# Decoding the first two expert weight blocks in two parts at the seam between attention and the expert layers

## The chip, the cores and the metric

The kernel runs on one core of one Trainium2 chip. The metric is the device time of one execution in microseconds; lower is better. A core has TensorE (PE, with its weight loads shown as PEld), VectorE (DVE), ScalarE (ACT), GpSimd (POOL) and SyncE (SP, which here only issues DMAs).

## The reference

A clustered attention feeds two expert layers, all in float32.

```python
# q, k, v: (2, 8, 768, 64); centroids: (8, 16, 64)
mask = argmax(q_n . c_n) == argmax(k_n . c_n)      # same nearest centroid
attn = softmax(where(mask, q k^T / 8, -1e9))
x = (attn @ v) as 1536 tokens x 512
# layer 1: w_in 512x2048, w_out 2048x512
x = max(0.01 h, h) @ w_out   with h = x @ w_in
# layer 2: same shapes
out = relu(h)**2 @ w_out     with h = x @ w_in
```

## The kernel before

**Numbers.** Every float32 product is made of three TensorE products of a high and a low part (`xh`, `xl`; `wh`, `wl`; `gh`, `gl`), so each operand is split: a copy rounds to the high part, a subtraction gives the low one.

**Attention.** There are 8 pairs of heads (NP), and each pair has 6 units (UPP) of 256 queries, 48 units (NU) in all. A unit has the scores `S` (line 438), their row maximum `nm` on DVE (460), the exponential `e` on ACT (470), the reciprocal `r` of the row sums (484), the normalisation on POOL (487), twelve transposes into PSUM `T` (500), the split of `T` into `eh` on ACT (511) and `el` on DVE (517), the product with the values into `A` (535), and the fold of `A` into `xt` on ACT (548) and DVE (557). When a pair is done, POOL splits `xt` into `xh` and `xl` (215, 565). `r_t[u]` holds a unit's row sums, `xt_t[p]` a pair's result.

**Experts.** 2048 hidden columns are taken in blocks of 128; a block is one tile of 128 x 1024 words, whose columns 0 to 511 are w_in and 512 to 1023 are w_out. The host passes each word as 64 bits of a wider format, so a block is a load `wraw` of 1024 KB (line 157) and a decode in seven pieces (`decode_pieces`): the load, `mag` on ACT (166), `shift`, `low` and `sign` on DVE (170, 176, 183), the high part `wh` on ACT and the low part `wl` on POOL (143, 144). There is one `wraw` buffer, so a block's load waits for the sign piece of the one before it.

For a pair of blocks, three groups of 512 tokens (b = 0, 1, 2) go through `unit(b, j)`: 12 matmuls of block j's w_in into one bank of `h` (line 865), then ACT and DVE split the activated result (908, 909, 914); and through `out_of(b, j)`: 12 matmuls of block j's w_out into four banks `o` (943). The first pair's sequence is unit(0,0), unit(0,1), unit(1,0), out_of(0,0), unit(1,1), out_of(0,1), unit(2,0), out_of(1,0), unit(2,1), out_of(1,1); the remaining two outputs come in the next pair's sequence. Group 0 needs attention pairs 0 to 3 alone; groups 1 and 2 need the last pair too, in the last three of a unit's 12 matmuls.

**Buffers.** PSUM has eight banks. The four of `h` are those of attention's `S`, three of `o` are those of `T`, and the fourth is that of `A`. SBUF of attention is given on, tile by tile, to pools opened after it. `stg[0]` holds `wraw` and one `wt`; `stg[1]`, opened after attention, another `wt` and `ws`.

**Order.** Attention up to its last six units is ordered by hand (`PLAN`). From there (`manual.close()`) the compiler's planner orders PE, DVE, ACT and POOL by its own model of the times, until `(m, f) == (0, 2)`, the second pair of blocks, where a hand order begins again (`order`). Instructions of a hand-ordered stretch keep their order among themselves on their engine; the planner places others around them. SP's DMAs keep the order in which they are written throughout. The pieces of the first block (`early`) are written one after another into attention's last six units; the pieces of the second after unit(0,0); its load is held, by a small POOL copy into its buffer, until the row sums of the third unit from the end exist. `TURN` says after which step of a pair which pieces of the next pair's blocks are written.

Of the kernel before, what the change touches and what calls it, by code (L numbers as in the profile page):

```python
# [18 lines left out]
W_SHIFT = float(2.0 ** -112)  # L19
# [45 lines left out]
def attention_moe_moe_kernel(  # L65
# [9 lines left out]
    nc = tc.nc  # L75
    NP, _, _, S = qk.shape
# [10 lines left out]
    N = 512  # L87
    NBLK = NT // N
    PLAIN = (3, 1)
    EARLY = 1  # L90
    RING = 6
    SIDE = 4

# [54 lines left out]
    def decode_pieces(ci):  # L148
# [3 lines left out]

        def load():
            st["raw"] = stg[0].tile([128, 2 * DM, 2], I32, tag="wraw", name="wraw")
            if ci == EARLY:
                pool_copy(out=st["raw"][:, 0].bitcast(F32), in_=r_t[NU - 3])
            nc.sync.dma_start(
                out=st["raw"].rearrange("p a b -> p (a b)"), in_=(w1, w2)[m][f + j].bitcast(I32)
            )

        def mag():
            pool = stg[0] if j == 0 or ci < 2 else stg[1]
# [26 lines left out]
            st["rest"] = split_block(ci, st["t"].bitcast(F32))  # L189

        return [load, mag, shift, low, sign, high, lambda: st["rest"]()]

    def sum_pieces(ci):

# [936 lines left out]
    def step_list(m, f, prev):  # L1131
# [30 lines left out]
        ((0, 1),), ((0, 2), (0, 3)), ((0, 4), (1, 0)), ((0, 5),), ((0, 6), (1, 1)),  # L1162
        ((1, 2), (1, 3)), ((1, 4), (2, 0)), ((1, 5), (1, 6), (3, 0)), ((2, 1),), ((2, 2),),
    )
    TURN_LAST = TURN[:9] + (
        TURN[9] + ((3, 1),), ((3, 2), (3, 3)), ((3, 4), (4, 0)), (),
    )
# [38 lines left out]
    for m in range(2):  # L1206
        turn = 0
        for f in range(0, NF, 2):
            if (m, f) == (0, 2):
                order.enter_context(  # L1210
                    tc.manual_schedule(
                        engines={
                            mybir.EngineType.PE,
                            mybir.EngineType.DVE,
                            mybir.EngineType.Activation,
                            mybir.EngineType.Pool,
                        }
                    )
                )
# [3 lines left out]
            for i, step in enumerate(seq):  # L1223
                step()
# [58 lines left out]
```

## Time and profile before

| | |
|---|---|
| time, median of 3 runs | 752.58 us (752.48 to 757.84) |
| the profiled execution: its own time | 753.01 us |
| its span, first to last instruction | 751.2 us |
| PE busy | 743.3 us, 99% |
| DVE, ACT, POOL busy | 573.1, 442.5, 404.7 us |

Matmul ends are modelled in the trace: a matmul of 512 columns shows as 390 ns but the next starts 227 ns after it, so starts and not busy times tell how dense PE is.

### The profile page before, as it was taken

Reading aid. Unit: us, or ns where it says so; the run is one execution under the profiler, and the core shown is the slowest. Engines: PE = TensorE matmul, PEld = TensorE weight load, DVE = VectorE, ACT = ScalarE, POOL = GpSimd, SP = SyncE. Lnnn points to the kernel's source line nnn. Section 1 sums busy time; section 2 is a strip of 40 time slices with the busy share of each in tenths; the row PEclk is TensorE's granted clock in tenths of the full one; section 3 lists DMA queues with packets and bytes.
Section 4 is the critical chain, followed back from the end, with each engine's and each line's share of the span. In section 5 each row is a group of like instructions: output and inputs, shape, how many; then the busy total and the mean of one; then the engine's idle time right before and its main releaser. Section 6 shows DMA issues by size and latency. Waiting matters only on the chain.

```text
span 751.2 us, 11081 instructions
## 1 busy us (share of the span) xinstructions
PE 743.3 (99%) x4044; PEld 647.6 (86%) x4044; DVE 573.1 (76%) x864; ACT 442.5 (59%) x816; POOL 404.7 (54%) x379
## 2 busy tenths in 40 slices
PE   9999999999989999999999999999999999999998
PEld 8999999999988888888888888888788888888886
DVE  7999999999998545877666576686868677686755
ACT  7988988988987564444444344547644445444430
POOL 6999999999856316551442414399242341423400
PEclk9999999999999999999999999999999999999999
DMA  3684574473503212111121112211112211122004
GB/s 108 174 215 113 117 175 114 114 175 74 151 0 113 87 38 101 56 57 57 60 110 57 56 57 63 106 57 56 57 57 84 84 57 56 57 89 79 1 1 168
DMA packets 16406, 64.78 MB, mean 86 GB/s; under 512 B 3040, under 2 KB 4192, under 8 KB 11360
## 3 DMA queue, kind: packets, MB, share of 16 engines
q1 hardware_dynamic: 16352, 64.07, 28.6%
q8 instruction: 32, 0.52, 0.3%
q14 instruction: 22, 0.18, 0.1%
HBM read 43.02 MB, written 3.15 MB: 61 GB/s over the span
## 4 chain that ended last, share of the span: by engine, by line
PE 90%; DVE 5%; ACT 4%; issue 1%; POOL 0%; DMA 0%; POOLq 0%; DVEq 0%; ACTq 0%
PE o L943 33%; PE h L865 32%; PE A L535 8%; PE S L438 7%; PE T L500 7%; ACT e L470 2%; PE S L311 1%; DVE nm L460 1%; DVE el L517 1%; ACT eh L511 1%; DVE xl L1127 1%; PE o L973 1%; PE dots L311 0%; DVE wt L176 0%; ACT wt L166 0%
## 5 line engine op out<-in xcount | busy, mean ns | idle before, releaser
L144 POOL TENSOR_TENSOR wl<-wt,wh 128x1024 fp32r<-128x1024 f32 x32 | 76.8, 2401 | 128.2 <-ACT wh L143 128.2
L914 DVE TENSOR_TENSOR gl<-h,gh 128x512 fp32r<-128x512 f32 x96 | 65.6, 690 | 71.2 <-ACT h L909 52.7
L865 PE MATMUL h<-xh,wh 128*128 128x512 f32 x288 | 112.2, 391 | 0.2
L865 PE MATMUL h<-xl,wh 128*128 128x512 f32 x288 | 112.2, 389 | 0.0
L865 PE MATMUL h<-xh,wl 128*128 128x512 f32 x288 | 112.0, 389 | 0.0
L985 DVE TENSOR_TENSOR acc<-o,acc 128x512 f32<-128x512 f32 x144 | 92.8, 684 | 12.8 <-PE o L943 12.8
L487 POOL TENSOR_SCALAR e<-e,r 128x768 f32<-128x768 f32 x96 | 89.0, 937 | 17.4 <-DVE r L484 13.2
L517 DVE TENSOR_TENSOR el<-T,eh 128x512 fp32r<-128x512 f32 x144 | 94.5, 682 | 3.3 <-ACT eh L511 2.0
L470 ACT ACTIVATE e<-S,nm 128x768 f32<-128x768 f32 x96 | 87.1, 908 | 11.2 <-DVE ds L339 5.2
L460 DVE TENSOR_REDUCE nm<-S 128x1 f32<-128x768 f32 x96 | 90.7, 947 | 3.9 <-PE S L311 2.0
L438 PE MATMUL S<-hb 128*128 128x384 f32 (+1 forms) x384 | 90.4, 350 | 1.3 <-ACT e L470 1.0
L511 ACT CAST eh<-T 128x512 fp32r<-128x512 f32 x144 | 79.7, 588 | 9.9 <-PE T L500 9.6
L500 PE MATMUL T<-ident,e 128*128 128x128 f32 x576 | 81.1, 274 | 0.9 <-POOL e L487 0.8
L535 PE MATMUL A<-eh,vv 128*128 128x256 f32 x288 | 80.0, 307 | 0.7 <-DVE xt L557 0.7
L207 POOL TENSOR_TENSOR ws<-wt 128x256 f32<-128x256 f32 x24 | 17.8, 741 | 110.8 <-DVE wt L183 110.8
L943 PE MATMUL o<-gl,wh 128*128 128x512 f32 x192 | 74.7, 389 | 0.0
L943 PE MATMUL o<-gh,wl 128*128 128x512 f32 x192 | 74.7, 389 | 0.0
L943 PE MATMUL o<-gh,wh 128*128 128x512 f32 x192 | 73.4, 389 | 0.0
L500 PEld LDWEIGHTS T<-ident,e 128*128 128x128 f32 x576 | 68.9, 143 | 5.1 <-POOL e L487 1.1
L535 PE MATMUL A<-el,vv 128*128 128x256 f32 x288 | 72.9, 283 | 0.0
L943 PE MATMUL o<-wh,gh 128*128 128x512 f32 x184 | 71.6, 389 | 0.0
L943 PE MATMUL o<-wl,gh 128*128 128x512 f32 x184 | 71.6, 389 | 0.0
(162 smaller groups left out, 1629.3 us busy)
## 6 DMA issues: line engine op xcount, KB each, us to landing
wraw<-w SPq DMA_DIRECT2D x32, 1024.0 KB, 4.7
hb<-spl SPq DMA_DIRECT2D x14, 576.0 KB, 4.7
hb<-spl SPq DMA_DIRECT2D x42, 192.0 KB, 5.1
rqk<-qk SPq DMA_DIRECT2D x16, 384.0 KB, 3.7
rv<-v SPq DMA_DIRECT2D x8, 384.0 KB, 3.2
out<-q SPq DMA_DIRECT2D x11, 256.0 KB, 2.0
hb<-st SPq DMA_DIRECT2D x56, 24.0 KB, 2.0
out<-q SPq DMA_DIRECT2D x2, 128.0 KB, 1.8
```

The lines of the kernel that those rows point to most:

```text
L144: return lambda: nc.gpsimd.tensor_tensor(out=wl, in0=t, in1=wh.bitcast(F32), op=ALU.subtract)
L438: nc.tensor.matmul(out=s[:, c, 0:HALF], lhsT=hb[0:k, a, i * 128 : (i + 1) * 128], rhs=hb[0:k, b, c * HALF : (c + 1) * HALF], start=(a == 0 ...
L460: nc.vector.tensor_reduce(out=n, in_=s_t[t][:, :, 0:HALF], axis=AX.XY, op=ALU.max, negate=True)
L470: nc.scalar.activation(out=e.rearrange("p (a b) -> p a b", a=2), in_=s_t.pop(t)[:, :, 0:HALF], func=AF.Exp, bias=n_t.pop(t), scale=1.0, ac ...
L487: nc.gpsimd.tensor_scalar(out=e_t[t], in0=e_t[t], scalar1=r_t[t // 2][:, t % 2 : t % 2 + 1], scalar2=1.0, op0=ALU.mult, op1=ALU.mult,)
L500: nc.tensor.transpose(T[:, o : o + 128], e_t[2 * u + b][:, kc * 128 : (kc + 1) * 128], ident)
L511: nc.scalar.copy(out=eh[:, 2 * g : 2 * g + 2, :].rearrange("p a b -> p (a b)"), in_=T_t[u, g])
L517: nc.vector.tensor_tensor(out=el[:, 2 * g : 2 * g + 2, :].rearrange("p a b -> p (a b)"), in0=T_t.pop((u, g)), in1=eh[:, 2 * g : 2 * g + 2, ...
L535: nc.tensor.matmul(out=A, lhsT=w, rhs=m[:, kc, :], start=(kc == 0 and i == 0), stop=(kc == KC - 1 and i == 1),)
L865: nc.tensor.matmul(out=out, lhsT=l, rhs=r, start=(first and i == 0), stop=(i == n - 1), skip_group_check=not first,)
L943: nc.tensor.matmul(out=outs[o], lhsT=l, rhs=r, start=(first and i == 0), stop=(last and i == 2),)
L985: nc.vector.tensor_tensor(out=a, in0=ps, in1=a, op=ALU.add)
```

## The change

The first two blocks of layer 1 are no longer decoded whole. `first_pieces(part)` decodes one half of a block: part 0 is w_in, part 1 is w_out, 512 KB each. The halves of part 0 (blocks 0 and 1) share one `wraw` buffer, of which the second is held by the copy from `r_t[NU - 3]`. The w_out half of block 0 then takes that buffer again; the w_out half of block 1 has buffers of `stg[1]`, and its load is held by a POOL copy from columns 256 to 257 of the last pair's `xt`, which the last unit but one writes. The pieces are written so: w_in of block 0 in attention's last six units; after unit(0,0), w_in of block 1, w_out of block 0, and the load of the third block; before step 3 of the first pair, out_of(0,0), the w_out of block 1. The hand order begins at that step 3 instead of at the second pair, and the first pair's sequence has a table of its own, `TURN_FIRST`.

```diff
         def load():
             st["raw"] = stg[0].tile([128, 2 * DM, 2], I32, tag="wraw", name="wraw")
-            if ci == EARLY:
-                pool_copy(out=st["raw"][:, 0].bitcast(F32), in_=r_t[NU - 3])
...
+    def first_pieces(part):
+
+        st = {}
+        cols = slice(part * DM, (part + 1) * DM)
+
+        def load(b):
+            if (part, b) == (1, 1):
+                raw = stg[1].tile([128, DM, 2], I32, tag="ws", name="wraw")
+                t = stg[1].tile([128, 2 * DM], I32, tag="wt", name="wt")[:, 0:DM]
+                pool_copy(out=raw[:, 0].bitcast(F32), in_=x_end[0][:, 256:258])
+            else:
+                if "raw" not in st:
+                    st["raw"] = stg[0].tile([128, 2 * DM, 2], I32, tag="wraw", name="wraw")
+                    st["t"] = stg[0].tile([128, 2 * DM], I32, tag="wt", name="wt")
+                h = slice(b * DM, (b + 1) * DM)
+                raw, t = st["raw"][:, h], st["t"][:, h]
+            st["views", b] = raw, t
+            if (part, b) == (0, 1):
+                pool_copy(out=raw[:, 0].bitcast(F32), in_=r_t[NU - 3])
+            nc.sync.dma_start(
+                out=raw.rearrange("p a b -> p (a b)"),
+                in_=w1[b].bitcast(I32)[:, 2 * cols.start : 2 * cols.stop],
+            )
...
-    early = [f for i in range(EARLY) for f in decode_pieces(i)]
+    first = [first_pieces(i) for i in range(2)]
+    early = first[0](0)
...
+    x_end = [xt_t[NP - 1]]
     xsplit(NP - 1, 0)
     xsplit(NP - 1, 1)
...
+    TURN_FIRST = (
+        (), (), (), ((0, 1), (0, 2), (0, 3)), ((0, 4), (1, 0), (0, 5)), ((0, 6),), ((1, 1),),
+        ((1, 2), (1, 3)), ((1, 4),), ((1, 5), (1, 6), (3, 0)),
+    )
...
-            if (m, f) == (0, 2):
-                order.enter_context(
...
             for i, step in enumerate(seq):
+                if (m, f, i) == (0, 0, 3):
+                    order.enter_context(
...
+                if (m, f, i) == (0, 0, 3):
+                    for g in first[1](1):
+                        g()
                 step()
                 if (m, f, i) == (0, 0, 0):
-                    for j in range(7):
-                        piece((0, 0, 1), j)
+                    for todo in (first[0](1), first[1](0)):
+                        for g in todo:
+                            g()
                     piece((0, 2, 0), 0)
-                table = {(0, NF - 2): TURN_LAST, (1, 0): TURN_SEAM}.get((m, f), TURN)
+                table = {(0, 0): TURN_FIRST, (0, NF - 2): TURN_LAST, (1, 0): TURN_SEAM}.get(
+                    (m, f), TURN
+                )
```

The other pieces of `first_pieces` (mag, shift, low, sign, high and the subtraction) are those of `decode_pieces` on 512 columns.

## Rows read from the trace of the kernel before

**Rows 1.** The page's part 1: busy time, share, instructions.

```profile
PE 743.3 (99%) x4044; PEld 647.6 (86%) x4044; DVE 573.1 (76%) x864; ACT 442.5 (59%) x816; POOL 404.7 (54%) x379
```

**Rows 2.** Chain of waits in order of time: start, duration, work.

```profile
268.43 2.72 PE h L865 x12
```

**Rows 3.** Busy time by stretch: length, then PE, PEld, DVE, ACT, POOL, clock, DMA.

```profile
210.00:215.00 5.00, 3.98 (x29) 3.46 (x28) 4.94 (x9) 3.96 (x10) 0.52 (x1) 1.00 0.00 0
215.00:220.00 5.00, 3.93 (x29) 3.18 (x27) 4.91 (x7) 4.57 (x11) 4.61 (x4) 1.00 0.00 0
```

**Rows 4.** Timeline of PE: start, duration, instruction, [idle before, releaser].

```profile
199.72 0.60 PE L500 MATMUL T<-ident,e 128*128 128x128 f32 x4
200.08 0.36 PE L535 MATMUL A<-eh,vv 128*128 128x256 f32 x1
...
211.21 0.63 PE L500 MATMUL T<-ident,e 128*128 128x128 f32 x4
212.86 0.97 PE L438 MATMUL S<-hb 128*128 128x384 f32 x4 [1.02 <-ACT e L470]
...
216.24 0.27 PE L500 MATMUL T<-ident,e 128*128 128x128 f32 x1
217.29 0.98 PE L500 MATMUL T<-ident,e 128*128 128x128 f32 x7 [0.78 <-POOL e L487]
218.44 0.38 PE L535 MATMUL A<-eh,vv 128*128 128x256 f32 x1 [0.17 <-DVE xt L557]
...
232.92 0.98 PE L500 MATMUL T<-ident,e 128*128 128x128 f32 x5
234.00 0.50 PE L865 MATMUL h<-xh,wh 128*128 128x512 f32 x1
...
252.60 0.40 PE L943 MATMUL o<-gh,wh 128*128 128x512 f32 x1
```

**Rows 5.** Timeline of all engines: the first block's decode.

```profile
207.70 1.17 ACT L166 ACTIVATE wt<-wraw 128x1024 f32<-128x1024 f32 x1
...
208.91 0.69 DVE L170 TENSOR_SCALAR wt<-wt 128x1024 int32<-128x1024 int32 x1 [0.25 <-ACT wt L166]
...
210.98 1.21 DVE L176 SCALAR_TENSOR_TENSOR wt<-wraw,wt 128x1024 int32<-128x1024 int32 x1
...
214.82 1.65 DVE L183 SCALAR_TENSOR_TENSOR wt<-wraw,wt 128x1024 int32<-128x1024 int32 x1
...
216.50 1.05 ACT L143 CAST wh<-wt 128x1024 fp32r<-128x1024 f32 x1
```

**Rows 6.** The page's part 5: busy, mean ns of one, idle before.

```profile
L914 DVE TENSOR_TENSOR gl<-h,gh 128x512 fp32r<-128x512 f32 x96 | 65.6, 690 | 71.2 <-ACT h L909 52.7
```

**Rows 7.** Groups of instructions by line, 260 to 500 us, columns as in rows 6.

```profile
L1086 ACT CAST th<-q 128x512 fp32r<-128x512 f32 x6 | 3.7, 610 | 0.0
L1083 POOL TENSOR_TENSOR t<-q 128x512 f32<-128x512 f32 x2 | 2.6, 1288 | 0.0
```

**Rows 8.** Busy time of line 865 alone, from attention's last exponential to its end.

```profile
233.90:252.55 18.65, 12.94 (x51) 9.28 (x51) 1.00 0.20 65
```

**Rows 9.** Timelines of ACT, DVE and POOL where attention ends.

```profile
244.66 1.14 ACT L166 ACTIVATE wt<-wraw 128x1024 f32<-128x1024 f32 x1 [2.71 <-DMA wraw<-w]
...
248.88 0.43 DVE L557 TENSOR_TENSOR xt<-A,xt 64x256 f32<-64x256 f32 x1
...
255.01 1.86 POOL L565 TENSOR_TENSOR xl<-xt,xh 128x768 fp32r<-128x768 f32 x1
```

**Rows 10.** POOL's timeline: the copy that holds the second block's load.

```profile
228.75 0.19 POOL L215 TENSOR_SCALAR wraw<-r 128x2 f32<-128x2 f32 x1
```

**Rows 11.** The page's part 6: DMAs, KB each, us from issue to landing.

```profile
wraw<-w SPq DMA_DIRECT2D x32, 1024.0 KB, 4.7
...
rv<-v SPq DMA_DIRECT2D x8, 384.0 KB, 3.2
...
hb<-st SPq DMA_DIRECT2D x56, 24.0 KB, 2.0
```

More of the change, by code (lines that the diff above doesn't have):

```diff
@@ L161, in mag @@
         def mag():
-            pool = stg[0] if j == 0 or ci < 2 else stg[1]
+            pool = stg[0] if j == 0 else stg[1]
             t = pool.tile([128, 2 * DM], I32, tag="wt", name="wt")
@@ L191, in decode_pieces, with of, views, mag @@
         return [load, mag, shift, low, sign, high, lambda: st["rest"]()]
+    def first_pieces(part):
[19 more added lines that the diff above has]
+            )
+        def of(b):
+            def views():
+                return st["views", b]
+            def mag():
+                raw, t = views()
+                nc.scalar.mul(out=t.bitcast(F32), in_=raw[:, :, 1].bitcast(F32), mul=W_SHIFT)
+            def shift():
+                t = views()[1]
+                nc.vector.tensor_scalar(
+                    out=t, in0=t, scalar1=3, scalar2=None, op0=ALU.logical_shift_left
+                )
+            def low():
+                raw, t = views()
+                nc.vector.scalar_tensor_tensor(
+                    out=t, in0=raw[:, :, 0], scalar=29, in1=t,
+                    op0=ALU.logical_shift_right, op1=ALU.bitwise_or,
+                )
+            def sign():
+                raw, t = views()
+                nc.vector.scalar_tensor_tensor(
+                    out=t, in0=raw[:, :, 1], scalar=-0x80000000, in1=t,
+                    op0=ALU.bitwise_and, op1=ALU.bitwise_or,
+                )
+            def high():
+                if part == 0:
+                    pool = next(q for q, n in ring if b < n)
+                    weights[0, 0, b] = tuple(
+                        pool.tile([128, 2 * DM], F32R, tag=x, name=x) for x in ("wh", "wl")
+                    )
+                wh, wl = (x[:, cols] for x in weights[0, 0, b])
+                t = views()[1].bitcast(F32)
+                nc.scalar.copy(out=wh, in_=t)
+                st[b] = lambda: nc.gpsimd.tensor_tensor(
+                    out=wl, in0=t, in1=wh.bitcast(F32), op=ALU.subtract
+                )
+            return [lambda: load(b), mag, shift, low, sign, high, lambda: st[b]()]
+        return of
@@ L1164, in attention_moe_moe_kernel @@
     )
+    TURN_FIRST = (
+        (), (), (), ((0, 1), (0, 2), (0, 3)), ((0, 4), (1, 0), (0, 5)), ((0, 6),), ((1, 1),),
+        ((1, 2), (1, 3)), ((1, 4),), ((1, 5), (1, 6), (3, 0)),
+    )
     TURN_LAST = TURN[:9] + (
@@ L1208, in attention_moe_moe_kernel @@
         for f in range(0, NF, 2):
-            if (m, f) == (0, 2):
-                order.enter_context(
[L1211 to L1219, printed above, removed]
             seq, prev = step_list(m, f, prev)
@@ L1223, in attention_moe_moe_kernel @@
             for i, step in enumerate(seq):
+                if (m, f, i) == (0, 0, 3):
+                    order.enter_context(
+                        tc.manual_schedule(
+                            engines={
+                                mybir.EngineType.PE,
+                                mybir.EngineType.DVE,
+                                mybir.EngineType.Activation,
+                                mybir.EngineType.Pool,
+                            }
+                        )
+                    )
+                if (m, f, i) == (0, 0, 3):
+                    for g in first[1](1):
+                        g()
                 step()
                 if (m, f, i) == (0, 0, 0):
-                    for j in range(7):
-                        piece((0, 0, 1), j)
+                    for todo in (first[0](1), first[1](0)):
+                        for g in todo:
+                            g()
                     piece((0, 2, 0), 0)
-                table = {(0, NF - 2): TURN_LAST, (1, 0): TURN_SEAM}.get((m, f), TURN)
+                table = {(0, 0): TURN_FIRST, (0, NF - 2): TURN_LAST, (1, 0): TURN_SEAM}.get(
+                    (m, f), TURN
+                )
                 for k, j in table[i] if i < len(table) else ():
```

1 line of the change is left out of this document (removed).

## The prediction

> **What bounds the kernel now.** I read the page's busy shares first. PE is busy 99% of the span [rows 1], so a gain can only come from places where PE's starts fall behind. Then the chain of waits: from 268 us on it is PE alone, 2.72 us for every 12 matmuls of the expert layers, 0.227 us each [rows 2]; nothing that leaves this pace alone can matter after 268 us. So I went through PE's timeline from 200 to 268 us and compared the distance between starts with the distance where PE is dense. Four transposes take 0.36 us when dense, 0.09 each. The four at 211.21 are followed by the next start after 1.65 us, 1.29 too late; the one at 216.24 after 1.05, 0.96 too late; the seven at 217.29 after 1.15, 0.52 too late; the five at 232.92 after 1.08, 0.63 too late [rows 4]. From 234.00 to 268 I find no start that lags by over 0.12 us. So this seam loses 2.8 us at 211 to 218 and 0.6 at 233, and that is all there is to gain: 3.4 us, 0.45%.
>
> Who makes PE late there? In the two stretches from 210 to 220 DVE is busy 4.94 and 4.91 of 5 us, ACT 3.96 and 4.57, POOL 0.52 and 4.61, PE 3.98 and 3.93 [rows 3]: DVE is the engine without slack. Into this stretch falls the decode of the first expert block: 1.17 and 1.05 us on ACT, and 0.69 + 1.21 + 1.65 = 3.55 us on DVE [rows 5].
>
> **Part 1: half a decode under attention.** Only w_in of block 0 is now decoded there. A DVE instruction over 512 columns with two tensors takes 0.69 us [rows 6], so the low and sign pieces fall from 1.21 and 1.65 to 0.69 each, 1.48 us less; the shift falls from 0.69 to between 0.35 and 0.69. DVE is relieved of 1.5 to 1.8 us. ACT, at 0.61 us for 512 columns [rows 7], is relieved of 2.22 - 1.22 = 1.0 us. As DVE has no slack there, I count what it is relieved of one for one on PE: -1.5 us. The ends: -2.8, if the shorter pieces dissolve all three stalls; and +1.3, since the planner sorts these pieces anew and may put one where it makes another stall like the largest one of now. The halves that were taken out run later on ACT, DVE and POOL beside dense PE work, at no cost if parts 2 and 3 hold.
>
> **Part 2: less work for PE to fill attention's end with.** From the last exponential to 252.60 PE runs 51 h matmuls between attention's last transposes and products [rows 8]: 12 + 12 + 9 + 9 + 9 of units (0,0), (0,1), (1,0), (1,1), (2,0); the missing threes need the last pair. In the new order unit(1,1) stands behind out_of(0,0), whose banks are those of `T` and come free with attention's last `el`. Before that only 12 + 12 + 9 = 33 are to be had, 18 fewer, 18 x 0.227 = 4.1 us. So PE stays dense only if attention's end comes 4.1 us sooner than PE now reaches it. It has room: three whole blocks are decoded or begun between 234 and 257 us, and one mag piece held ACT 2.71 us for its DMA, in front of attention's copies [rows 9]. After the change two halves stand there, one block's worth instead of two: on DVE 0.69 + 2 x 1.21 = 3.1 us less by the durations of rows 5 (the sign's without its stretch), and a load of half the size lands 0 to 1.5 us sooner [rows 11]. Together 3.1 to 4.6 us sooner against the 4.1 needed. I take 0.3 us of loss; the ends are 0 (no gain is possible where PE is dense) and 4.1, all of the missing filler. Behind the last product the fold and split up to 256.87 [rows 9] took 4.3 us from 252.60; for that stretch out_of(0,0) and nine matmuls of unit(1,1) are there, 21 x 0.227 = 4.8 us, just enough.
>
> **Part 3: the w_out half of block 1.** It is due when PE comes to out_of(0,1), after 60 expert matmuls (36 of h in three units, 12 of out_of(0,0), 12 of unit(1,1)) instead of the 51 at 252.60: 252.60 - 1.5 + 9 x 0.227 = 253.1 us. Its load waits for a POOL copy of 0.19 us [rows 10], which waits for the fold of the last unit but one, now done at 249.31 [rows 9]. With 1.5 us from part 1 and 0 to 4.1 from part 2 that is 243.7 to 247.8. No row shows a load of 512 KB: 384 KB land in 3.2 us, 1024 KB in 4.7 [rows 11], so between these; 3.7 us is where a straight line between them puts it. Then mag 0.6, shift 0.35, low and sign 0.69 each and the copy 0.6 (halves of rows 5, rows 6, rows 7): 2.9 us. The high part is there between 243.7 + 0.2 + 3.2 + 2.9 = 250.0 and 247.8 + 0.2 + 4.7 + 2.9 = 255.6; the low part 1.29 us later [rows 7], due only two matmuls after the high one. The middle, 252.8, is just in time, so I take 0; the ends are 0 and 2.5 us. On SP this load also stands behind the third block's 1024 KB, and moving those takes 4.7 - 2.0 = 2.7 us by the 1024 KB and 24 KB rows [rows 11]; if both go out together the end is 5.2. Behind the waiting instructions on ACT, DVE and POOL stand the third block's pieces and unit(1,1)'s split; they are later due than out_of(0,1), so the wait is paid once.
>
> Rows of 384 and 1024 KB alone can't say how much of a load is fixed. The Trainium skill (DMA: Bandwidth & Descriptors, Anatomy of one DMA) gives about 2.0 us for every DMA and the bytes at 436 GB/s on top, which speaks against cutting a load in two: 3.2 us for 512 KB as an estimate by that page, 4.4 for 1024 KB where the trace has 4.7. By it part 3's landing would be at its early end, and the sum the same.
>
> **Part 4: the rest.** One more POOL copy of 0.19 us, two more DMAs, and the fourth and fifth blocks' pieces two steps (5.4 us) later in `TURN_FIRST` than `TURN` had them. The fourth block is due at the second unit of the next pair, two g2 groups after its last piece; I cost it at nothing. If that cover is gone it is one wait of the size of the 2.71 us seen for a DMA [rows 9]. The hand order from 268 us on is otherwise the old one.
>
> **The sum**, against the profiled execution's own 753.01 us (span 751.2 plus 1.8 around it): -1.5 + 0.3 + 0 + 0 = 751.8. That execution stands 0.43 above the median of the runs shown, so 751.4 us is what I predict for the median.
>
> **The rivals.**
>
> *Slower, the late second half.* The w_out half lands later than 253.1 - 2.9 = 250.2 us, and PE, whose order is fixed there, waits before out_of(0,1) with nothing else to run. For it: the load is held by one of attention's last folds and stands behind 1024 KB on SP. Against it: attention's end should come sooner. From 2.5 to 5.2 us, 3.9 in the middle: 751.4 + 3.9 = 755.3.
>
> *Nothing comes of it.* ACT, 4.57 of 5 us busy at 215 to 220 [rows 3], or POOL behind it takes DVE's place, or part 2 gives back the 1.5 us: about 752.6. The hold from the last unit but one may also never be what ends last, since SP's order already keeps that load behind the third block's; then it does nothing for the time.
>
> *All of it.* The stalls at 211 to 218 and the one at 233 vanish and nothing is late: 752.58 - 3.4 = 749.2.
>
> **How the numbers follow.** Forecast 0.42 (750.5 to 752.2), nothing 0.18 (752.2 to 753.3), late half 0.27, all of it 0.13. Faster cases and no change hold most of the chance, but half of the slower case must be covered: the range runs from 749.2 to 755.4, which leaves out about half of the late cases and half of the best ones. Within 1% (7.5 us) is about what a measurement of this kernel can't tell from no change. Faster by more is excluded by the 3.4 us that PE loses, but for noise: 0.01. Slower by more needs both ends, 4.1 + 5.2 us: 0.03. Within: 0.96. So the likely verdict is no difference, with a sign that favours faster.
>
> **What would show it.** Part 1: in the changed kernel's PE timeline the distances behind the transposes near 211 and 217 us shrink to a sum of about 1.3 us, and the first h matmul, at 234.00 now, comes near 232.5. Part 2: no start lags between the last exponential and the first o matmul; if one does, before the o, with `el` as releaser, the filler was short. Part 3: PE's waits name no ACT or POOL of the new decode lines; if they do at the 13th o matmul, the late half is right. Part 4: 12 matmuls in 2.72 us from about 266 us on, as now. The prediction is wrong if the planner's new order of attention's last units makes stalls where there are none now, which no row of before can show, or if the hand order's earlier start keeps PE from work that it now takes out of turn.

## The result, and the profile after

The changed kernel takes 757.1 us (median of 20 executions), the kernel before 752.6 beside it: ratio 1.006, 95% interval [1.0042, 1.0078]. The prediction of 751.4 us is wrong, in sign and beyond its upper end of 755.4. Now and then an execution of most kernels of this study takes some 5 us more (2 of 20 of before, 3 of 20 here); the ratios count these, and the medians hardly feel them.

The page's part 1 of the changed kernel, against [rows 1]:

```profile
PE 744.7 (99%) x4044; PEld 648.1 (86%) x4044; DVE 575.3 (76%) x870; ACT 443.2 (59%) x820; POOL 402.8 (53%) x382
```

The share of PE is 99% as before, while the span went from 751.2 to 755.5 us: a busy share says nothing of 4.3 us in 750. PE's timeline does (columns as in [rows 4]; lines 566, 601, 933, 1011 are 500, 535, 865, 943 of before):

```profile
205.39 1.48 PE L566 MATMUL T<-ident,e 128*128 128x128 f32 x12
...
210.05 1.04 PE L566 MATMUL T<-ident,e 128*128 128x128 f32 x8
212.03 0.39 PE L601 MATMUL A<-eh,vv 128*128 128x256 f32 x1 [0.94 <-DVE xt L623]
...
231.49 0.48 PE L933 MATMUL h<-xh,wh 128*128 128x512 f32 x1
...
243.74 0.60 PE L566 MATMUL T<-ident,e 128*128 128x128 f32 x4
246.69 0.38 PE L601 MATMUL A<-eh,vv 128*128 128x256 f32 x1 [2.35 <-DVE xt L623]
...
248.71 0.63 PE L1011 MATMUL o<-gh,wh 128*128 128x512 f32 x1
249.14 0.63 PE L1011 MATMUL o<-gl,wh 128*128 128x512 f32 x1
...
255.72 0.39 PE L933 MATMUL h<-xh,wl 128*128 128x512 f32 x1
257.36 0.50 PE L1011 MATMUL o<-gh,wh 128*128 128x512 f32 x1 [1.25 <-ACT wh L250]
...
258.72 0.50 PE L1011 MATMUL o<-gh,wl 128*128 128x512 f32 x1 [0.63 <-POOL wl L251]
```

Four places, each read as the distance between starts less the dense distance. The first h matmul comes at 231.49 where it came at 234.00: 2.5 us gained; of the stalls near 211 to 218 and 233 in [rows 4] one of 1.26 us is left, at 210. Behind the transposes of 243.74, PE waits 2.6 us for attention's fold `xt` (2.35 as the profile gives it in brackets, from the modelled end of the last transpose). Then the o matmuls stand 0.43 us apart instead of 0.227. And before the 13th o matmul PE waits twice, 1.41 and 0.79 us, for the late w_out half of block 1. The second and third go with a fallen clock, as busy time by stretch shows (columns as in [rows 3]; the third number from the end is the granted clock, of which 1.00 is the 2.4 GHz level):

```profile
240.00:245.00 5.00, 4.34 (x29) 3.70 (x28) 3.03 (x6) 2.93 (x7) 1.05 (x1) 1.00 0.17 29
245.00:250.00 5.00, 3.31 (x16) 3.02 (x17) 2.72 (x5) 1.68 (x4) 0.54 (x3) 0.76 0.74 288
250.00:255.00 5.00, 5.00 (x21) 4.10 (x20) 3.03 (x3) 0.67 (x1) 2.54 (x2) 0.90 0.00 1
255.00:260.00 5.00, 3.12 (x13) 1.93 (x13) 2.29 (x3) 3.61 (x6) 1.28 (x1) 1.00 0.00 0
```

The matmul distance of 0.43 us, 1.9 times 0.227, goes with the 1.2 GHz level. From 247.65 to 251.15 PE runs at it, and loses 1.6 us by the distances. The sum: -2.5 + 2.6 + 1.6 + 2.2 = +3.9, and some 0.3 of small lags, against 4.3 of the spans. From 264 us on 12 matmuls take 2.72 us as in [rows 2].

Not all of the 2.5 us is the change's. In the kernel before, the twelve transposes that start at 205.39 in the changed kernel, before the decode of the first block begins, start here:

```profile
205.99 1.48 PE L500 MATMUL T<-ident,e 128*128 128x128 f32 x12
```

So 0.6 us is there before the change can act (attention's first scores start at 10.04 us there and at 9.28 here). In the 18 runs below, whose attention is that of the changed kernel, these transposes start anywhere from 205.43 to 206.35, but from them to the first h matmul it is 26.1 us in each, as in the changed kernel (231.49 - 205.39), and 28.0 in the kernel before. The early half is worth 1.9 us, and 0.6 us is a difference between two executions.

Who makes attention's fold late? The timeline of ACT and DVE around it:

```profile
239.56 0.66 ACT L220 ACTIVATE wt<-wraw 128x512 f32<-128x512 f32 x1 [1.43 <-DMA wraw<-w]
...
242.54 0.68 DVE L237 SCALAR_TENSOR_TENSOR wt<-wraw,wt 128x512 int32<-128x512 int32 x1
243.25 0.62 ACT L250 CAST wh<-wt 128x512 fp32r<-128x512 f32 x1 [2.07 <-DVE wt L237]
...
243.78 0.59 ACT L976 ACTIVATE gh<-h 128x512 fp32r<-128x512 f32 x1
...
244.78 0.59 ACT L577 CAST eh<-T 128x512 fp32r<-128x512 f32 x1
...
245.40 0.36 ACT L614 COPY xt<-A 64x256 f32<-64x256 f32 x1
...
246.21 0.43 DVE L623 TENSOR_TENSOR xt<-A,xt 64x256 f32<-64x256 f32 x1
```

ACT stands 1.43 us before a mag that waits for its load, then 2.07 us before a cast that waits for DVE's sign piece. Behind them in its order come `gh`, `h`, `eh`, and only then attention's fold `xt` at 245.40, whose second half on DVE ends at 246.64, 0.05 us before PE goes on. Two decode pieces that were not yet due held the engine.

And the late half, in the timeline of ACT, DVE, POOL and SP:

```profile
246.83 0.19 POOL L281 TENSOR_SCALAR wraw<-xt 128x2 f32<-128x2 f32 x1 [1.62 <-DVE xt L623]
247.05 0.33 SPq L209 DMA_DIRECT2D wraw<-w  x1
...
250.56 0.67 ACT L220 ACTIVATE wt<-wraw 128x512 f32<-128x512 f32 x1 [1.25 <-DMA wraw<-w]
250.78 1.85 POOL L631 TENSOR_TENSOR xl<-xt,xh 128x768 fp32r<-128x768 f32 x1
251.26 1.65 DVE L224 TENSOR_SCALAR wt<-wt 128x512 int32<-128x512 int32 x1 [1.49 <-ACT wt L220]
...
253.72 0.69 DVE L237 SCALAR_TENSOR_TENSOR wt<-wraw,wt 128x512 int32<-128x512 int32 x1
255.69 0.60 ACT L976 ACTIVATE gh<-h 128x512 fp32r<-128x512 f32 x1 [4.46 <-PE h L933]
...
256.70 0.60 ACT L250 CAST wh<-wt 128x512 fp32r<-128x512 f32 x1
...
257.38 1.28 POOL L251 TENSOR_TENSOR wl<-wt,wh 128x512 fp32r<-128x512 f32 x1 [4.75 <-ACT wh L250]
```

The words are whole at 254.41. The cast could then run on an idle ACT and be done at 255.0, before PE wants it at 255.95; but by the hand order it stands behind `gh` and `h` of the unit whose last matmul starts at 255.72, so it begins at 256.70. ACT was idle for 4.46 us in front of it.

### The profile page after: what moved, and what is told of

It reads as the page before. It is cut to its first block, busy times and chain, and to the rows that moved or that the text cites. A ratio compares the mean times of both kernels' runs of the same rounds, so it can differ in the third digit from the quotient of the medians.

```text
span 755.5 us, 11095 instructions
## 1 busy us (share of the span) xinstructions
PE 744.7 (99%) x4044; PEld 648.1 (86%) x4044; DVE 575.3 (76%) x870; ACT 443.2 (59%) x820; POOL 402.8 (53%) x382
## 4 chain that ended last, share of the span: by engine, by line
PE 85%; DVE 6%; ACT 4%; DMA 2%; issue 1%; POOL 1%; DVEq 0%; ACTq 0%; POOLq 0%; SPq 0%
PE o L1011 32%; PE h L933 29%; PE A L601 8%; PE S L504 7%; PE T L566 7%; DMA wraw<-w 2%; PE S L377 1%; ACT e L536 1%; DVE nm L526 1%; DVE el L583 1%; PE o L1041 1%; PE warm L318 1%; ACT eh L577 1%; DVE wt L180 0%; ACT wt L163 0%
## 5 line engine op out<-in xcount | busy, mean ns | idle before, releaser
L143 POOL TENSOR_TENSOR wl<-wt,wh 128x1024 fp32r<-128x1024 f32 x30 | 72.1, 2402 | 127.1 <-ACT wh L142 127.1
L553 POOL TENSOR_SCALAR e<-e,r 128x768 f32<-128x768 f32 x96 | 86.7, 914 | 14.5 <-DVE r L550 10.3
L1011 PE MATMUL o<-gh,wh 128*128 128x512 f32 x192 | 75.5, 393 | 1.4 <-ACT wh L250 1.2
L1011 PE MATMUL o<-wh,gl 128*128 128x512 f32 x184 | 71.6, 389 | 0.0
```

The lines of the kernel that those rows point to most:

```text
L143: return lambda: nc.gpsimd.tensor_tensor(out=wl, in0=t, in1=wh.bitcast(F32), op=ALU.subtract)
L553: nc.gpsimd.tensor_scalar(out=e_t[t], in0=e_t[t], scalar1=r_t[t // 2][:, t % 2 : t % 2 + 1], scalar2=1.0, op0=ALU.mult, op1=ALU.mult,)
L1011: nc.tensor.matmul(out=outs[o], lhsT=l, rhs=r, start=(first and i == 0), stop=(last and i == 2),)
```

## The experiments

The kernel before took 752.5 to 753.0 us (medians) beside these runs. "Lost" is the sum, from 205 to 305 us, of PE's distances between starts beyond the dense ones (0.09 us for a transpose, 0.18 and 0.12 in attention's products, 0.227 in the expert layers); before loses 6.0 by that count and the changed kernel 10.6. The waits of the last column are as the profile gives them in brackets, 0.1 to 0.3 us under the same waits read by distance. `acc` is the buffer into which ACT copies and DVE adds the finished banks `o`; PE waits for it where it needs such a bank again.

| run | edit | median us | ratio, 95% interval | lost us | PE's long waits there |
|---|---|---|---|---|---|
| e1 | hand order from the second pair on | 760.4 | 1.0095 [1.0061, 1.0129] | 12.9 | `wh` 4.5, `acc` 2.4 |
| e2 | two units moved ahead of out_of(0,0) | 760.5 | 1.0084 [1.0055, 1.0113] | 13.5 | `wh` 2.8, `acc` 1.9, `wl` 0.6, `xl` 0.4 |
| e3 | late half not held | 755.8 | 1.0043 [1.0016, 1.007] | 9.7 | `xt` 2.3, `acc` 0.5 |
| e4 | w_out cast on POOL | 754.6 | 1.0018 [0.9996, 1.0039] | 7.7 | `wl` 1.5, `xt` 1.0, `wh` 0.5 |
| e7 | late half left out (block 0's w_out in its place) | 755.0 | 1.0025 [1.0007, 1.0044] | 8.3 | `xt` 2.2 |
| e15 | e3 + e4 | 754.6 | 1.0034 [1.0022, 1.0045] | 7.3 | `wl` 1.5, `xt` 1.0, `wh` 0.5 |
| e5 | e2 + e3 + e4 | 756.7 | 1.0045 [1.0028, 1.0062] | 9.8 | `acc` 1.9, `wl` 1.1, `wh` 0.7 |
| e6 | e2 + e4 | 756.8 | 1.0048 [1.0027, 1.007] | 9.8 | as e5 |
| e8 | e5, late half loaded before the third block | 759.1 | 1.006 [1.0034, 1.0085] | 11.7 | `wl` 1.7, `wh` 0.8 |
| e9 | all halves in one buffer, no hold | 757.2 | 1.0059 [1.0038, 1.008] | 10.6 | `xt` 3.1 |
| e11 | e9 + w_out cast on POOL | 756.9 | 1.0059 [1.0036, 1.0081] | 9.9 | `xt` 2.4 |
| e10 | e9 + hand order from the second pair on | 754.5 | 1.0015 [0.9991, 1.0039] | 7.5 | `xl` 1.8, `gh` 0.9 |
| e12 | e10 + w_out cast on POOL | 754.5 | 1.0014 [0.9998, 1.003] | 7.5 | `xl` 1.9 |
| e13 | e10 + third block's load held | 752.5 | 1.0004 [0.9992, 1.0015] | 6.1 | `acc` 1.4, `gl` 0.4 |
| e14 | e13, held by the last fold | 755.3 | 1.0042 [1.003, 1.0054] | 7.9 | `acc` 1.7, `wl` 1.4, `gl` 0.8 |
| e16 | e10 + third block's mag held | 752.1 | 0.9991 [0.9967, 1.0015] | 5.3 | `acc` 1.4 |
| e17 | e16 + one sign piece later | 751.4 | 1.0002 [0.9983, 1.0021] | 4.3 | `acc` 0.5 |
| e18 | e17 again | 751.6 | 0.9993 [0.9973, 1.0014] | 4.3 | `acc` 0.4 |

Every run with the early half also has the wait of 0.9 us at 210 (`xt`), which the table leaves out.

### Was it the missing filler?

Part 2 says that PE waits at attention's end because only 33 h matmuls are to be had there. e1 and e2 give them back, in two ways: e1 lets the planner place the whole first pair, e2 writes units (1,1) and (2,0) in front of out_of(0,0).

```diff
e1:
-                if (m, f, i) == (0, 0, 3):
+                if (m, f, i) == (0, 2, 0):
                     order.enter_context(
```

> The hand order begins at the second pair again, as before the change; halves, buffers, hold and piece table stay. Filler theory: PE lost attention's end because out_of(0,0) was put ahead of unit(1,1) and unit(2,0), so 33 instead of 51 matmuls were there to fill it; with them back the 2.6 us stall before the last product at 246.69 and the half clock behind it (1.6 us) go, and the wait for the second w_out half (2.2 us) may shrink: 750.7 to 753. ScalarE-order theory: attention's last copies stand on ACT behind a cast that waits for the decode, whatever PE does: the stall stays, 755 or more. Late-half theory: only the 2.2 us at out_of(0,1) matter and the rest is noise of the planner: 755 to 757.

```diff
e2:
+            if (m, f) == (0, 0):
+                seq = [seq[k] for k in (0, 1, 2, 4, 6, 3, 5, 7, 8, 9)]
...
-        (), (), (), ((0, 1), (0, 2), (0, 3)), ((0, 4), (1, 0), (0, 5)), ((0, 6),), ((1, 1),),
-        ((1, 2), (1, 3)), ((1, 4),), ((1, 5), (1, 6), (3, 0)),
+        (), (), (), (), (), ((0, 1), (0, 2), (0, 3)), ((0, 4), (1, 0), (0, 5)), ((0, 6), (1, 1)),
+        ((1, 2), (1, 3), (1, 4)), ((1, 5), (1, 6), (3, 0)),
...
-                if (m, f, i) == (0, 0, 3):
+                if (m, f, i) == (0, 0, 5):
```

> The hand order stays, but the first pair's sequence has unit(1,1) and unit(2,0) ahead of out_of(0,0), and the hand order begins at out_of(0,0) (step 5), the pieces moved along with it. Filler theory: 51 matmuls fill attention's end, no stall before the last product, clock 1.00 throughout; out_of(0,1) is 24 matmuls (5.4 us) of units further back relative to attention's end than the 33 of now, so the second w_out half is just in time: 750.5 to 752.5. ScalarE-order theory: the stall of 2 to 3 us before attention's last product stays: 754.5 or more. Late-half theory: 2.2 us better, 755.

In both the wait of 2.6 us at attention's end is gone and PE is dense up to 253 us, as Part 2 wants it, and both are 3 us slower than the change itself. PE only comes sooner to the next thing that isn't ready, and loses clock behind that wait too (0.56 from 260 to 265 us in e1, 0.50 in e2). In e1, PE and ACT in their timelines:

```profile
254.55 1.07 PE L933 MATMUL h<-xh,wh 128*128 128x512 f32 x4
260.13 0.80 PE L1011 MATMUL o<-gh,wh 128*128 128x512 f32 x1 [4.52 <-ACT wh L250]
```

```profile
248.10 1.14 ACT L163 ACTIVATE wt<-wraw 128x1024 f32<-128x1024 f32 x1 [1.22 <-DMA wraw<-w]
...
252.53 1.05 ACT L142 CAST wh<-wt 128x1024 fp32r<-128x1024 f32 x1 [2.20 <-DVE wt L180]
253.48 0.68 ACT L220 ACTIVATE wt<-wraw 128x512 f32<-128x512 f32 x1
259.46 0.62 ACT L250 CAST wh<-wt 128x512 fp32r<-128x512 f32 x1 [5.31 <-DVE wt L237]
```

The planner put the third block's mag and cast (248.10, 252.53), which are due later, in front of the late half's mag (253.48). So the wait at attention's end has filler as its condition, but filler is not what the time hangs on: this theory fell.

### Was it the late half?

e3 takes its hold away, e4 its cast from ACT, e7 the half itself.

```diff
e3:
-                pool_copy(out=raw[:, 0].bitcast(F32), in_=x_end[0][:, 256:258])
e4:
-                nc.scalar.copy(out=wh, in_=t)
+                (nc.scalar.copy if part == 0 else pool_copy)(out=wh, in_=t)
e7:
-        wh, wl = weights[m, f // 2 * 2, f % 2]
+        wh, wl = weights[m, f // 2 * 2, f % 2 if (m, f) != (0, 1) else 0]
...
-                if (m, f, i) == (0, 0, 3):
-                    for g in first[1](1):
-                        g()
```

> The POOL copy that holds the load of the second w_out half is taken out; the load then stands on SP right behind the third block's load, issued at 243.6 instead of 247.05 but behind 1024 KB. Filler theory: the stall before attention's last product stays, only the wait at out_of(0,1) shrinks, by 0.5 to 2.2 us: 755 to 756.6. Late-half theory: the hold is the whole loss: 753 or less.

> The high parts of the two w_out halves are cast on POOL instead of ACT, so that ACT no longer waits for their decode in front of attention's last copies (2.07 us idle at 243.25) nor casts the second one behind unit(1,0)'s activation at 256.7. ScalarE-order theory: the last eh copies come 1.5 to 2 us sooner, the stall before the last product falls from 2.6 to about 1 us or less, the clock stays at 1.00, and the wait at out_of(0,1) falls too: 752 to 754. Filler theory, strict: PE has nothing to run there in any case, as the rest of the chain is as long: 756 to 757.5.

> The changed kernel without the load and decode of block 1's w_out half: out_of(b,1) of the first pair uses block 0's w_out in its place, so that the output differs. What is left is the loss at attention's end. Two-waits theory: the wait at out_of(0,1), 2.2 us, is gone, the stall of 2.6 and the slow clock of 1.6 us stay: 754 to 755. If the second half alone makes the change slow: 750 to 751.

Without the half, the kernel takes 755.0 us: 2.1 us less than the change, the 2.2 of its two waits, and still 2.0 above the 753.0 of before beside it. The wait of 2.5 us at 244 and the clock behind it stay. The hold is worth about 1.3 us (757.1 to 755.8): the load goes out at 244.63 instead of 247.05 and the wait before the 13th o matmul shrinks to 0.4. In e4, where ACT no longer holds the w_out casts, the wait at 244 shrinks to 0.9 and the clock stays at 1.00, as the theory of ScalarE's order expected, though both other waits, now for POOL, add up to 2.3 us. That a cast on another engine shortens a wait of attention is the first sign of the theory below.

e15 joins e3 and e4; e5 and e6 join e2 and e4 with and without the hold; e8 also loads the late half ahead of the third block.

```diff
e8 (on e5):
                 if (m, f, i) == (0, 0, 5):
-                    for g in first[1](1):
+                    for g in second[1:]:
                         g()
...
+                    second = first[1](1)
+                    second[0]()
                     piece((0, 2, 0), 0)
```

> The change with its own order, the w_out casts on POOL and no hold (the two edits that helped each by itself, 755.8 and 754.6). Front-of-queue theory: the last eh copies still stand behind unit(0,1)'s activation, about 0.9 us; the half lands about 1 us sooner than with the cast alone, so the 2.3 us at out_of(0,1) fall to 1 to 1.5: 753 to 754. If the two edits save the same time: 754.6.

> unit(1,1) and unit(2,0) ahead of out_of(0,0), both w_out halves cast on POOL, and the second half's load not held. Two-waits theory (PE loses at two places that hand the time to each other: attention's end for want of matmuls and because of ACT's order, and out_of(0,1) for want of the second half, each with half clock behind it): all of its causes are gone, PE is dense from 231 to 262, the clock stays at 1.00 and only the 2.5 us won under attention are left: 750 to 751. Theory that the planner's order of attention's end is what costs: a stall moves elsewhere again, 754 or more.

> As the one before, but the hold on attention's last unit but one is kept. Two-waits theory: the high part is there at about 253.5 and the low part at 255.8, PE comes to out_of(0,1) at about 255.5: a wait below 0.5 us, 750 to 751.5. If the hold is what made the change slow: 753 or more with a wait at out_of(0,1) of over 2 us.

> As the first of these four, but the second half's load stands on SP ahead of the third block's 1024 KB instead of behind it. If SP's order delays the half: it lands 1 to 2 us sooner and, where out_of(0,1) still waited, the time falls by as much; two-waits theory has no wait left there: the same time as the first, 750 to 751, within 0.3.

Both causes together, by the theory of the expectations, leave 750 to 751.5 us for e5, e6 and e8, and these took 756.7 to 759.1. The savings don't add up: e15 is e4 again, with the same waits. e5 and e6 are equal, so the hold decides nothing there. Both have no wait at attention's end, and lose 1.2 and 2.1 us at 274 and 294, for pieces of the blocks behind. e8 brings the half sooner and the third block later, and PE then waits 2.5 us for that one in the second pair. In e1, e2, e5, e6 and e8 the time removed from one wait turned up in others; only e3, e4, e7 and e15 kept part of it.

### Is it what stands in front on ACT, DVE and POOL?

The theory that was left: the time is handed back by decode pieces that wait (for a load, or for each other) and stand, in an engine's fixed order, in front of attention's last copies and folds or of the sums into `acc`. e9 to e12 first take the late half's separate buffers, hold and place away: all four halves lie in one buffer, and their pieces are given to the planner together.

```diff
e9:
-        st = {}
+        st = whole
...
-            if (part, b) == (1, 1):
-                raw = stg[1].tile([128, DM, 2], I32, tag="ws", name="wraw")
-                t = stg[1].tile([128, 2 * DM], I32, tag="wt", name="wt")[:, 0:DM]
-                pool_copy(out=raw[:, 0].bitcast(F32), in_=x_end[0][:, 256:258])
...
-                    for todo in (first[0](1), first[1](0)):
+                    for todo in (first[0](1), first[1](0), first[1](1)):
e10 (on e9): hand order from (0, 2, 0) on as in e1, table TURN for the first pair
e11 (on e9), e12 (on e10): the cast of e4
```

> All four halves share one wraw tile and one wt tile: block 0's w_out half goes where its w_in half was (free since about 211 us), block 1's w_out half where block 1's w_in half was (free at about 236); no stg[1] buffers and no hold from the last unit but one; block 1's w_out pieces are written behind block 0's; the hand order still begins at step 3. Two-waits theory: the wait at out_of(0,1) is gone, the wait at attention's end stays in part (0.9 to 2.6 us), as the order of PE is the change's: 752 to 754.5. If buffers and hold were the whole cause: 750 to 751.5.

> As the one before, but the hand order begins at the second pair and TURN is used for the first pair as well, as before the change: what is left of the change is decoding in halves alone. Two-waits theory: both places are dense, only the gain under attention is left: 750 to 751.3. If the planner's new order of attention's end costs by itself: 753 or more.

> e9 with the two w_out halves cast on POOL. ACT-order part of the two-waits theory: the wait at attention's end shrinks to below 1 us as it did when the cast alone was moved: 751 to 752.5, below e9 by 0.5 to 1.6.

> e10 with the two w_out halves cast on POOL. Two-waits theory: nothing is left to gain, the same as e10 within 0.5: 750 to 751.3.

With the hand order kept (e9, e11) nothing is won: the wait at 244, 2.35 us in the changed kernel by its bracket, is 3.06 and 2.40. With the planner's order (e10, e12) PE is dense up to 258 us, and then waits 1.9 us for `xl`: 754.5 us where 750 to 751.3 were expected. The timelines of ACT, of DVE and of POOL in e10 show who is in front:

```profile
250.45 1.12 ACT L163 ACTIVATE wt<-wraw 128x1024 f32<-128x1024 f32 x1 [1.64 <-DMA wraw<-w]
251.60 0.36 ACT L611 COPY xt<-A 64x256 f32<-64x256 f32 x1
```

```profile
251.60 0.69 DVE L167 TENSOR_SCALAR wt<-wt 128x1024 int32<-128x1024 int32 x1 [2.06 <-ACT wt L163]
...
253.59 1.23 DVE L180 SCALAR_TENSOR_TENSOR wt<-wraw,wt 128x1024 int32<-128x1024 int32 x1
254.85 0.43 DVE L620 TENSOR_TENSOR xt<-A,xt 64x256 f32<-64x256 f32 x1
```

```profile
256.17 2.39 POOL L143 TENSOR_TENSOR wl<-wt,wh 128x1024 fp32r<-128x1024 f32 x1
258.52 1.80 POOL L628 TENSOR_TENSOR xl<-xt,xh 128x768 fp32r<-128x768 f32 x1
```

Attention's last fold, two instructions of 0.36 and 0.43 us, stands behind the third block's mag on ACT, which waited 1.64 us for its load, and behind that block's three pieces on DVE. On POOL that block's low piece of 2.39 us then stands in front of the `xl` that PE waits for. If it is the order, then a hold that keeps these pieces behind the fold frees PE, whatever it holds. e13 holds the block's load by a copy from the fold of the last unit but one, e14 by one from the last fold, e16 lets the load go and holds the mag.

```diff
e13 (on e10):
+            if ci == 2:
+                pool_copy(out=st["raw"][:, 0].bitcast(F32), in_=x_end[0][:, 256:258])
             nc.sync.dma_start(
e14: the same with x_end[0][:, 512:514]
e16 (on e10), in mag():
+            if ci == 2:
+                pool_copy(out=t[:, 0:2].bitcast(F32), in_=x_end[0][:, 512:514])
```

> e10 (halves in one tile, the planner's order for the whole first pair) with one more POOL copy: the third block's load is held until the last unit but one is folded, so that the planner puts its mag and DVE pieces behind attention's last fold. Front-of-queue theory: in e10 the last product ended at 250.05 but its fold on DVE only at 255.28, behind the third block's mag (which waited 1.64 us for its DMA) and its three DVE pieces; without them in front the last pair's split ends at about 253.5 instead of 260.3, PE is dense up to the second pair and only the gain under attention is left: 750 to 751.5. Rival, that decode in halves is too much work for this place whatever its order: 753.5 or more.

> As the one before, but held until the last unit itself is folded: the load goes out about 3 us later. Front-of-queue theory: attention's end is as free as in the one before, but the third block is late for the second pair's first unit by 1 to 3 us: 751.5 to 754. If lateness of weights does not matter there: the same as the one before within 0.3.

> The kernel of e10 (all halves in one tile, hand order from the third block pair on), with one more POOL copy that holds the third block's mag, not its load, until attention's last fold. Theory of the front of the queue: what matters is not when the third block's load goes out but that its pieces stand in front of attention's last folds on ACT and DVE. Then PE stays dense up to 265 us as in e13, the 1.9 us wait for POOL's xl at 258 us of e10 is gone, and because the load is not late the waits of e13 in the second pair (0.6 at 265 and 1.5 at 291 us) shrink too: 751 to 752.5 us, ratio 0.998 to 1.000. Rival, the hold itself is what helped in e13 by taking traffic away from attention's end: then this kernel, with its load as early as e10's, has e10's 1.9 us wait again and 754.5 us. Rival, the stall is only pushed along: PE dense to 265 us, but 2 us or more lost at the waits for the third or fourth block behind it, 753 to 754.5 us.

e13 is 2.0 us faster than e10 (medians) and stands where before stands: PE is dense from 216 to 265 us. Its late load costs 0.6 us at 265 and 1.5 at 291; held longer, in e14, that cost grows, to 4.4 us in three places. e16 has the order without the late load. Its timeline of ACT, DVE and POOL:

```profile
250.03 0.36 ACT L613 COPY xt<-A 64x256 f32<-64x256 f32 x1 [1.42 <-PE A L600]
251.98 1.14 ACT L165 ACTIVATE wt<-wraw 128x1024 f32<-128x1024 f32 x1 [1.58 <-POOL wt L280]
```

```profile
250.43 0.43 DVE L622 TENSOR_TENSOR xt<-A,xt 64x256 f32<-64x256 f32 x1 [1.09 <-ACT xt L613]
253.16 1.16 DVE L169 TENSOR_SCALAR wt<-wt 128x1024 int32<-128x1024 int32 x1 [2.30 <-ACT wt L165]
```

The fold is done at 250.86 instead of 255.28, the mag comes behind it, and between 216 and 290 us no start of PE lags by over 0.13 us. One wait is left, of 1.41 us at 291.61, and DVE's timeline names the same cause, a sign piece in front of four sums:

```profile
286.33 2.20 DVE L175 SCALAR_TENSOR_TENSOR wt<-wraw,wt 128x1024 int32<-128x1024 int32 x1
...
289.65 1.21 DVE L182 SCALAR_TENSOR_TENSOR wt<-wraw,wt 128x1024 int32<-128x1024 int32 x1
290.78 2.47 DVE L1052 TENSOR_TENSOR acc<-o,acc 128x512 f32<-128x512 f32 x4
```

The kernel before has the same pieces at almost the same times, but there PE comes later, and finds the sums done (its next o matmul starts at 292.75, without a wait). e17 puts that sign piece, (1, 4) of the table, one step later in the second pair; e18 runs the same kernel again.

```diff
+    TURN_SECOND = TURN[:6] + (((2, 0),), ((1, 4), (1, 5), (1, 6), (3, 0))) + TURN[8:]
...
-                table = {(0, NF - 2): TURN_LAST, (1, 0): TURN_SEAM}.get(
+                table = {(0, 2): TURN_SECOND, (0, NF - 2): TURN_LAST, (1, 0): TURN_SEAM}.get(
```

> The kernel of e16 with one more edit: in the second block pair the sign piece of one decode (DVE, 1.21 us, at 289.65 in e16) stands one step later in the hand order, behind the four sums into acc that PE waited 1.41 us for. Theory of the front of the queue: PE's last wait of this seam is the sign piece in front of those sums, so it goes; PE is then dense from 216 us on, the time is that of e16 less 1.2 to 1.4 us, 750.7 to 750.9 us, ratio 0.997 to 0.998. What the early half saves (2.5 us by the first h matmul, less 0.3 to 0.6) is then kept. Rival, the sign piece's own block is what comes late next: its cast on ACT and its subtraction on POOL move 2.4 us back, PE waits 1 to 2 us for one of them some matmuls later, and the time is 752 to 753 us as in e16.

> The kernel of e17, unchanged. In e17, 8 of 12 executions took 750.65 to 751.61 us, below each of the 17 of the kernel before beside them (752.49 to 753.40), but 4 took 756.03 to 756.28. Theory: these 4 are the extra of about 5.4 us that now and then falls on every kernel here, before included, and have nothing to do with the edit; then some 1 to 3 of 12 show it here, and the others lie at 750.7 to 751.7 us again, 1.5 us below those of before. Rival: the edit itself makes the extra more frequent; then 4 or more of 12 show it again and none or few of before, and the gain is not one.

DVE in e17:

```profile
290.22 2.46 DVE L1052 TENSOR_TENSOR acc<-o,acc 128x512 f32<-128x512 f32 x4
292.61 1.21 DVE L182 SCALAR_TENSOR_TENSOR wt<-wraw,wt 128x1024 int32<-128x1024 int32 x1
```

The wait falls from 1.41 to 0.46 us and nothing comes late in its place: the span is 749.5 us, 1.7 below that of before, as the lost time is (4.3 against 6.0). As its twelve transposes start at 205.93, like those of before (205.99), the two spans can be set side by side: 1.7 of the 1.9 us that the early half is worth are kept. Whether that kernel is the faster one is not settled: of its 24 executions in e17 and e18 17 took 750.65 to 751.72 us, below each of 33 of before beside them (752.49 to 753.60); 7 took the 5 us more, and 1 of 34 of before did. Over the whole study 20 of 180 executions of before did. e18's own 3 of 12 are what its theory expected, but 7 of 24 leave its rival open. The intervals hold 1, and what sets off the longer executions wasn't found.

## Why the prediction was wrong

**Part 1 was right, and too small.** -1.5 us was forecast and -1.9 came, within its ends (-2.8 to +1.3). The first h matmul stands at 231.49 where "near 232.5" was expected, but 0.6 us of that is luck of the execution, there at 205 us already. One stall of 1.26 us stayed; a sum of about 1.3 was expected.

**Part 2 is the step that failed.** Its loss of 0.3 us (ends 0 to 4.1) was 2.6, and the clock's 1.6 on top. Two things were wrong in it. First, the relief: 3.1 to 4.6 us were set against the 4.1 needed, and next to nothing of it came. The fold `xt` that PE waits for ended at 246.64, against 249.31 in [rows 9]. That is 2.7 us sooner, but the first h matmul had come 2.5 us sooner too, so that counted from there the fold gained 0.2 us. Before the change PE reached attention's last product 1.9 us after that fold:

```profile
251.17 0.28 PE L535 MATMUL A<-eh,vv 128*128 128x256 f32 x1
```

These 1.9 and 0.2 us are all that the 4.1 us of missing filler had to set against, and what they don't cover, 2.0 us, is most of the wait. (The last pair's split, with `xl` at 250.78 against 255.01 in [rows 9], did come 4.2 us sooner, but PE was not waiting for that here.) Second, the relief was counted as work taken off DVE and ACT, when what holds these engines is waiting: 1.43 and 2.07 us of idle ACT in front of two decode pieces of 0.6 us each. The row that showed this was at hand, the mag of 2.71 us in [rows 9], but it entered the sum only as a load that lands 0 to 1.5 us sooner. The sign that the prediction gave for short filler, a lag before the first o matmul released by `el`, did not come: the lag stands before the last product and is released by `xt`. And e1 and e2 showed that the filler is not what the time hangs on.

**The clock was left out.** The prediction has no term for it, since the kernel before ran at 1.00 in every stretch, stalls of 1.3 us included. The 20 executions of the changed kernel give its price: 8 with a mean clock of 1.000 took 755.9 to 756.9 us (median 756.2), 9 with 0.998 took 756.9 to 757.8 (median 757.4), the three longer ones aside. So it costs 1.2 us where it falls (1.6 by the distances of the one traced execution), and the change would be slower by 3.6 without it.

**Part 3: the size was within its ends, the path to it was not.** Forecast 0, ends 0 to 2.5 (5.2 behind the 1024 KB load); it cost 2.2, and 2.1 by e7. That this lies within the ends is luck: PE came to out_of(0,1) at 255.95, 2.8 us after the forecast's 253.1, and the high part was there at 257.30, 1.7 us after the latest of its times (255.6). The load itself was quicker than the 3.7 us taken: 3.4 us. The Trainium skill (DMA: Bandwidth & Descriptors, Anatomy of one DMA) gives 3.2 us for 512 KB as an estimate by that page, whose fit is for DMAs issued on GpSimd; this one, issued on SyncE, agrees within 0.2. Going out behind the third block's load cost little, since that one had gone out 3.8 us before: the half loaded at 236.32 took 3.2 us. What was mis-sized is the 2.9 us for five pieces, which took 6.7 from the mag to the end of the cast (250.56 to 257.30): the shift 1.65 us instead of 0.35, and the cast 2.3 us behind a finished sign, because `gh` and `h` stood in front of it on ACT. The sentence "the wait is paid once" named what is queued behind the waiting instruction, and never what the new pieces themselves are queued behind.

**The rivals.** "Slower, the late second half" had the place and the price of the last two waits, and 755.3 us; it lacked the wait at attention's end, and no rival joined the two, though part 2's end and part 3's end together would have reached 757.7. What e17 and e18 show can be had, 1.1 to 1.7 us, is the size of the forecast (1.2) and less than half of the 3.4 of "All of it".

**What is shown, and what isn't.** That decode pieces in front of attention's folds and of the sums into `acc` hand the time back is shown by e13, e16 and e17, which change little but the order and lose 1.4, 2.2 and 3.2 us less than e10. For the changed kernel itself, with its hand order from the fourth step on, the same cause is read from ACT's timeline, and e4 supports it; no run mended that kernel by order alone. Which part of its 4.5 us is the hand order's and which the planner's stays open: handing the first pair back to the planner made the changed kernel 3.3 us slower (e1), and the kernel with one buffer 2.7 us faster (e9 to e10).

## What to carry to other kernels

When an early piece of work is made shorter, the engine that it frees reaches every later due time sooner: set each later relief against the gain already counted, and walk on through the next waits until one has slack of that size. In an in-order queue look at idle time in front of instructions that aren't urgent, above all those that wait for a load: they cost whatever stands behind them. Holding one such piece was worth 2.4 us here (e10 to e16), where taking casts off ACT in an order otherwise left alone was worth 0.2 and nothing (e9 to e11, e10 to e12), and 2.5 in the one place where the cast itself had ACT waiting (e4). When a wait disappears, ask what PE meets next before counting it as gain; e1 and e2 removed the wait that was blamed and were 3 us slower.

## What the hardware showed that was not expected

**TensorE's clock after a wait.** After the wait of 2.6 us at 244 the granted clock was 0.76 and 0.90 in the next two stretches of 5 us, and in e1, after 4.7 us, 0.56 from 260 to 265. After 2.0 us in e12 it was 0.66 from 260 to 265; after 1.9 us in e10's traced execution, 2.1 us at 294 in e5, and waits of 1.3 to 1.9 us in the changed kernel, e13, e14 and e16, it stayed at 1.00. The length of the wait alone doesn't settle it: by the mean clocks of the executions it fell in 12 of 20 of the changed kernel, in 9 of 12 of e10 and in 7 of 11 of e12, and in e8 it was 0.66 from 275 to 285 behind waits of 0.8 and 1.7 us at 274 and 276. So a wait near 2 to 2.6 us may or may not cost the clock on top.

**DVE beside POOL's subtraction.** DVE instructions whose operands all lie in SBUF, such as the decode pieces, end only after a POOL instruction on two tensors beside which they start, by their own usual length less 0.12 to 0.15 us. The shift of 251.26, usually 0.43 us, ended 0.28 us after POOL's `xl`; e16's shift of 253.16, usually 0.69, ended at 254.32, 0.55 after the `xl` there, which these rows of POOL in e16 give:

```profile
251.91 1.86 POOL L630 TENSOR_TENSOR xl<-xt,xh 128x768 fp32r<-128x768 f32 x1
...
285.70 1.74 POOL L1156 TENSOR_TENSOR tl<-q,th 128x512 fp32r<-128x512 f32 x1
```

The low piece of 286.33, usually 1.21 us, took 2.20 and ended 1.09 us after the `tl` of the second row. Instructions that read PSUM (`gl`, `el`, `xt`, `nm`) are not stretched: a `gl` at 244.89 in the changed kernel took its 0.69 us beside a POOL subtraction that ran until 245.21. In the traces of before, the changed kernel, e10 and e16 from 200 to 320 us it comes out so for all 31 DVE instructions of the first kind that stand in a row of their own, tiny reciprocals of two columns aside, and for all 57 of the second. The Trainium skill (GPSIMD Engine Reference, Specifications) says that GpSimd shares its interfaces to the buffer with VectorE and that instructions with two inputs there contend, among others; the low pieces, with two inputs in SBUF, and `gl`, with one, agree. The price here is up to the whole rest of POOL's instruction, which the prediction's durations, all but the first block's sign from undisturbed rows, left out.
